# Transposing P through DMA for three of four head groups, and through TensorE into two banks for the last

## The chip, the cores and the metric

The kernel runs on one core of one Trainium2 chip. The metric is the device time of one execution in microseconds (us), as the median of several runs. The kernel before has a median of 2704.88 us in 3 runs (2704.35 to 2705.86).

## The reference

Two layers, and each is an attention block followed by a gated feed-forward block (FFN). The input is x with 2048 tokens of 576 numbers. The attention is recurrent: the tokens come in 64 segments of 32, and each segment sees 8 memory rows ahead of its own 32.

```python
for s in range(64):                                   # layer A, called twice
    h = concatenate([mem, layernorm(x)[32*s:32*s+32]])          # 40 rows
    q, k, v = h @ Wq, h @ Wk, h @ Wv                            # 32 heads of 128
    p = softmax(where(mask, q @ k.T * 128**-0.5, -1e9))         # 40 x 40 for each head
    o = (p @ v) @ Wo
    mem = o[:8]; out[32*s:32*s+32] = o[8:]
x = x + out                                           # then layer B, FFN of width 4608
x = x + (silu(layernorm(x) @ w1) * (layernorm(x) @ w3)) @ w2
```

`mem` of one segment enters the next, so the segments of one layer can't run side by side. Both layers have the same weights.

## The kernel before, in words

**Steps.** Layer 2 runs `LAG = 8` segments behind layer 1, so there are 72 steps, and step `t` works on segment `t` of layer 1 and segment `t - 8` of layer 2. In the 56 steps with both layers (8 to 63) the 40 rows of either layer lie beside each other: 80 columns go through the projections with one load of the weights. In the other 16 steps one layer is there alone. The FFN of four finished segments (128 tokens of one layer, or of both) is cut into 18 pieces that are laid between the attention steps; their weights come by DMA from the queue of SyncE (SP) in two buffers each (`W13`, `W2C`).

**One step.** The 32 heads go in `NG = 4` groups of `GH = 8`. For each group, in the letters of the order (below): `Q` and `q` are the projections to Q and K and their 64-row tails; evictions to `QKT`; `S` the scores, 8 heads by up to two layers, into one bank (layer 1 in partitions 0 to 39, layer 2 in 64 to 103); VectorE (DVE) adds the mask, takes the maximum and subtracts it, ScalarE (ACT) takes the exponential in place (`SME`), DVE sums, inverts, and writes the quotient to `PB` in bf16, each layer's rows at the columns that are the rows of V that they need (`sm_pb`, three or four pieces, as `p_at` says). The other columns of `PB` must be zero.

**The transposition of P** is letter `T` (`ptr`, L1015): eight matmuls of 40 columns with `PB` of one head as the weights and `fold` as the moving operand. `fold` adds the rows of both layers on top of each other, so that one bank holds the sum for all eight heads; two evictions (`pt_ev`, L1022) copy the bank twice to `PTS` and multiply each by a column of `slots`, which is 1 in the partitions of one layer and 0 elsewhere. So the layers are parted again. GpSimd (POOL) then clears that `PB` buffer (`pb_zero`, L1009) once for each group; there are two `PB` buffers and one `PTS`.

**After it**: `P` multiplies V by `PTS` into two banks (`pv`), which are evicted to `OT`; `O` and `o` multiply `OT` by Wo and sum all four groups in one bank (`wo`, `wo_tail`). At the step's end `y_odd`, `y_mem` and `yts` carry the memory rows to the next step's `HT` and the outputs to `YTS`, which letter `p` (`post_tr`) transposes once in four steps. `F`, `f`, `W`, `w` are the FFN, `V`, `v`, `X`, `x`, `G`, `g` the projections to V.

**What sets the order.** `make_nodes` (L232) describes all work as nodes with an engine, a cost, dependencies and buffer slots. The order of TensorE's nodes is written out: `ORDER = FIRST + FOUR * 11 + LAST` (L222), one letter for each node, where `FOUR` holds four steps and repeats eleven times (44 of the 56 steps with both layers). `plan` (L75) takes TensorE's nodes in just that order and lays the nodes of the other engines and the DMAs beside them by its costs; nodes of kind `AD` (evictions) go to ScalarE or VectorE, whichever it finds free first. Each engine then does its own nodes strictly in this order (`ch`, L579): an instruction that waits holds up all that stand behind it on its engine. A matmul node for which the planner chose the mode `col` is issued in two halves of 64 output rows each (`mm`, L586), which changes the number of matmuls and not the work. A change between modes (128 rows, 64 row halves, column halves or quarters) is a change of tile shape on TensorE.

**DMA queues.** Weights and `XN` go out on SP, residuals and results on POOL, and in the kernel before ScalarE issues four DMAs at the very start only.

Of the kernel before, what the change touches and what calls it, by code (L numbers as in the profile page):

```python
# [34 lines left out]
POOLS = {"bank": 8, "qkt": 4, "sme": 2, "pb": 2, "pts": 1, "ot": 4,  # L35
# [158 lines left out]
def ewh(*ns):  # L194
# [5 lines left out]
    "maQQQqqQqqSQqTqSqQQQqSSvVXxPTPTOPOTOoPooOoQqqqqQQSQqqvSVQQTQSqqPQOTSPoXTOPToxPOOooQqqqqQQSQQSvqVQTqqQSQqPSaOTPTO"  # L200
    "PTooPOOooQQqqqqQSQVvSqqQQQqqQTSSPXTOPTOPoToxPOOooQQpQqqVvqqSnQQSfFFqqfQQqSTQqfPFTWPSFTOOooPFTffPOOooWQqqqqQQFSQF"
    "SQffqVvqqQWTQSFxfqfQFSPXTWPFTfOPOTFPOOooooWQqfqQQSFQfqqVvSQqqfFWTQqfQSFPQqfTOSPFOTWPFTOPfoooOoFfqqQQQSWQqqvVSFfq"
    "qQQTWqqSQQPTSOoPbaOTXPxTOPooxOoXqqpQQQSVqqnQvfFSTQqqQQPSFfqqfQTFOPSWTFfPOOTFPWOooooffFQQQqqqWSGFfgqQQqfFSTQPQQqq"
    "qfFSWGTSfgGPFggTGOPOTFPOOooooWVvfqqQQQSFqqffFQQWTSFfqqQPQfqqSFQWTOfPSTaFoOPWOTFPffFOoooWQQqqqqQSbQgqqGSQQTQPQTgq"
    "qSGSOPGggTGPOTOPoooOoQqqppQQQSvqqVnnQQqqSFSffqTFQPQqWTFSPffOwTFPOTFPOWOwooooFffqqQQQSWwQFfgqqGSFqqfQQTWQPQSFffqq"
    "FGTgSwPGfggTGPFTOPOWOOowoooFqqfQQwWQaQfqqSFSvVfqqQFQTFqqfPQTQwSWFSfPOOTFPwTWffFPOOooooWwqqqQQQbSQqqgqGSQTQPQQqgq"
    "TSGSGPggGTOPOTOPoooOo"
)
FOUR = (
    "QqqpQQpQqqVvnSSnQFfqfqFQQQTfqqSFPWTFPSwTfFOOPWTwPOOooooFqqffQQQQfqqSFGSgqfFTQQPwQTQqqqgGSWPFGSfggfFOTGPOwTOPWOoo"  # L210
    "ooFqfqqQQwWQQVqvSaSFFffqqQQwQQqqSTWSFPffTFOPWwTOFPffTOFPwWOooooFfqqqQQWQQSqqqQSQQbQqgqSTGGPSgTGPOTggGPOTwPOOoooo"
)
LAST = (
    "QQpQqqqQSqQpnQqqVvTSSnQFffqqFPQTOwPoSWTffFPFTOPOOoooFqqqfQQwWQQfqfSFSFqGQQqqgTQQPWwFqgfTSSGGPFfggfFTGOPOTWPOOwoF"
    "oooFfqqfQQQwvSqqVQQWQqqSFTSqfqQPQWTOPSwFTFPffOTOwPWOooooFFqqffQQwQQqqvSWVSFqqfQQTWPQTqqSVQvPOSTbOPxwOoTooPOoXqQp"
    "QpqqvVQSQqqnQnSQQqqFTSfqfPQTOPSFTFPOWTOPwOooooFqffqQQQSQQqqqvVSTQQqqFSffqFPQWSwTFPffTOPFOTwPOOoWoooFqfqqQQQFSQfq"
    "xvXVwWSTFPQffqqQWQTSwFFPfqqQOSwWTFOPffTFPOWOwooooFQQvfqqVqqQSQWFSwFffqqQQQSTWQqPqTPSOTOPowOToboPxOoXqqqQQQpSvVqq"
    "qQQSnQTFfqQFSPfqQOSTFfPowTFPfOTOPFOfooowQQqqqfQQSqFSVvqqQwQFTSQffqqQPFTSXPwTOPOTFPOOooooFfxfVvqqQQQSQqqqfQSFQqqq"
    "QSTQwSPFTOffPFTOPwTOPfooOooFQqqqQQSqqqQQSQvVQTSfFQqqPwTFSPfTOFPOTOPoofOoopwFnfffFFwFwfffFFFwffFFwffFFwffFFwfFffF"
    "wFwfffFFFfww"  # L220
# [11 lines left out]
def make_nodes(em, nseg, pools, o=Opt, dma_bw=230e3, load_bw=400e3):  # L232
# [26 lines left out]
    ld_m0 = node("ACT", 0.1, em.load_m0(), prio=-90, name="m0", lat=2.5)  # L259
    ld_t = [load("ldt", kb(3 * R64, 4096), -10.0, em.load_tails(0)), node("ACT", 0.1, em.load_tails(1), prio=-120, name="ldt", lat=6.0)]  # L260
    node("ACT", 0.1, em.load_tails(2), prio=-80, name="ldt", lat=6.0)
# [48 lines left out]
    def v_nodes(name, t, k, prio, tail_at, emit, strips, deps, tail_deps, free):  # L310

        modes = ("col", "quad") if strips[0][3] == R64 else ("c32", "oct")
        b = banks()
        m_ = node("PE", 8 * 0.2158, emit(b, False), deps=deps, prio=prio, mode=modes[0], acq=b, name=name)
        n = node("PE", 0.2158, emit(b, True), deps=deps + tail_deps, prio=prio + tail_at, mode=modes[1], acq=b, name=name + "t")
        reads_ht.setdefault(t, []).extend([m_, n])
        for r in (0, 1):
            outs = em.v_parts(strips, r)
            b[r].users = len(outs)
            for p0, width, row, blk in outs:  # L320
                e = node("AD", (0.49, 0.6), em.v_ev(b[r], p0, width, row, blk), deps=[m_, n] + free.get(blk // 2, []), prio=prio + 0.01 * (blk // 2),
                         rel=[b[r]], name=name + "e")
                vx_ev.setdefault((name, t, blk // 2), []).append(e)
        return [m_, n]
# [16 lines left out]
    def vg_out(t, g, b, deps, row):  # L341

        return [node("AD", (0.49, 0.6), em.v_ev(b[r], row, R64, row, 2 * g + r), deps=deps, prio=t + o.vm + 0.01 * g + (0.05 if row == 0 else 0.0), rel=[b[r]],
                     name="VGe") for r in (0, 1)]

    def vx_pair(t, prio):
# [5 lines left out]
        for k in ((0, 1) if both(t) else (0,)):  # L352
            v_nodes("VX", t, k, prio + 0.01 * k, o.vxt, (lambda k: lambda b, tail: em.vx(t, k, b, tail))(k), em.vx_strips(t, k), deps, [], free)

    def step(t):
# [17 lines left out]
        for g in range(NG):  # L373
# [22 lines left out]
            pb = Slot("pb")  # L396
            d = node("DVE", 0.623 if nl == 2 else 0.606, em.sm_sum(t, g, sme), deps=[c], prio=pf, name="sum")
            w = (1.074 if e else 1.143) if nl == 2 else 0.466
            pbs = node("DVE", w, em.sm_pb(t, g, sme, pb), deps=[d], prio=pf, acq=[pb], rel=[sme], name="pb", lat=0.125 if nl == 2 else 0.225)
            pts = Slot("pts")  # L400
            bt = Slot("bank", users=2)
# [24 lines left out]
            me[f"SC{g}"], me[f"TR{g}"], me[f"PV{g}"], me[f"WO{g}"] = sc, tr, pv, wo  # L426
# [100 lines left out]
    def x_in(g):  # L527
        xn = Slot("xn")
        ld = node("DMA" if g else "ACT", 0.8 if g else 0.1, em.load_xn(g, xn), deps=reads_ht.get(4 * g - 3, [])[:1], prio=4 * g - 3.0 if g else -100, acq=[xn],
                  name="ldxn", lat=2.5)  # L530
# [31 lines left out]
SW = 2 * QW  # L562

# [4 lines left out]
class Emitter:  # L568
# [431 lines left out]
    def sm_pb(self, t, g, sme, pb):  # L1000
        def f(n):
            for kd, key, c0, w in self.p_at(t):
                rs = slice(64 * kd, 64 * kd + QW)
                X, rec = self.T.SME[rs, sme.i], self.T.STAT[rs, sme.i]
                self.v("tensor_tensor", self.T.PB[rs, pb.i, :, c0:c0 + w], X[:, :, key:key + w],
                       rec.unsqueeze(2).to_broadcast([QW, GH, w]), op=ALU.mult)
        return f

    def pb_zero(self, pb):  # L1009
        return lambda n: self.ch("POOL", self.nc.gpsimd.memset(self.T.PB[:, pb.i], 0.0))  # L1010
# [4 lines left out]
    def ptr(self, t, g, pb, b):  # L1015

        def f(n):
            for j in range(GH):
# [3 lines left out]
    def pt_ev(self, t, g, m, b, pts):  # L1022

        def f(n):
            src = self.bk(b)[:, 0:GH * QW]
            if not self.both(t):
                w = 4 * QW
                self.cp(n, self.T.PTS[:, pts.i, 0, m * w:(m + 1) * w], src[:, m * w:(m + 1) * w])
                return
            dst = self.T.PTS[:, pts.i, m, :]  # L1030
            keep = self.T.slots[:, role(t), m ^ role(t):(m ^ role(t)) + 1]
            if n.by == "ACT":
                self.act(dst, src, ACT.Copy, scale=keep)
            else:
                self.v("tensor_scalar", dst, src, keep, None, op0=ALU.mult)
        return f

    def pv(self, t, g, pts, b):
        def f(n):
            nq = self.nq(t)  # L1040
            for j in range(GH):
                self.mm(self.bk(b[j // 4])[:, (j % 4) * nq:(j % 4 + 1) * nq], self.T.V[:, self.head(g, j) // 4, (self.head(g, j) % 4) * E:(self.head(g, j) % 4 + 1) * E],
                        self.T.PTS[:, pts.i, 0:nq // QW, j * QW:(j + 1) * QW], True, True)
        return f

# [66 lines left out]
    def yts(self, t, ls, tail):  # L1112
        def f(n):
            yT, _ = self.yT(t)
            for li in ls:
                j = (t - LAG * li) % 4
                c0 = self.ycol(t, self.kind(t, li), False)
                if not tail:
                    self.cp(n, self.T.YTS[:, li, 0:4, j * SEG:(j + 1) * SEG], yT[:, 0:4, c0:c0 + SEG])
                else:  # L1120
                    self.v("tensor_tensor", self.T.YTS[R64:P, li, 4, j * SEG:(j + 1) * SEG], yT[0:R64, 4, c0:c0 + SEG],
# [3 lines left out]
    def post_tr(self, li, g, b):  # L1125
        def f(n):

            for db in (4, 3, 2, 1, 0):
                d0 = min(db * P, D - P)
                self.mm(self.bk_bf(b, D)[:, d0:d0 + P], self.T.YTS[:, li, db, :], self.T.ident[:, 0:P], True, True, is_transpose=True)  # L1130
# [79 lines left out]
def kernel(  # L1210
# [41 lines left out]
    T.fold = sp.tile([P, QW], BF, name="fold")  # L1252

    T.slots = sp.tile([P, 2, 2], F32, name="slots")

# [13 lines left out]
    T.PB = sp.tile([P, pools["pb"], GH, P], BF, name="PB")  # L1269
# [15 lines left out]
    nc.gpsimd.memset(T.fold[:], 0.0)  # L1285
    for r in (0, R64):
        nc.gpsimd.affine_select(out=T.fold[:], in_=T.fold[:], compare_op=ALU.not_equal, fill=1.0, base=-r,
                                pattern=[[-1, QW]], channel_multiplier=1)

    nc.gpsimd.memset(T.slots[:], 0.0)  # L1290
    for e, kd, lo, hi in ((0, 1, 24, 80), (1, 0, 72, 112)):
        inside, outside = T.slots[:, e, kd:kd + 1], T.slots[:, e, 1 - kd:2 - kd]
        nc.gpsimd.memset(inside, 1.0)
        nc.gpsimd.affine_select(out=inside, in_=inside, compare_op=ALU.is_ge, fill=0.0, base=-lo, pattern=[[0, 1]], channel_multiplier=1)
        nc.gpsimd.affine_select(out=inside, in_=inside, compare_op=ALU.is_ge, fill=0.0, base=hi - 1, pattern=[[0, 1]], channel_multiplier=-1)
        nc.gpsimd.tensor_scalar(outside, inside, -1.0, 1.0, op0=ALU.mult, op1=ALU.add)

# [54 lines left out]
```

## Time and profile before

| | us |
|---|---|
| median of 3 runs (lowest, highest) | 2704.88 (2704.35, 2705.86) |
| the profiled execution | 2708.0 |
| its span, first to last instruction | 2705.0 |
| TensorE (PE) busy in the span | 2618.6 |
| VectorE (DVE) busy | 2097.7 |
| ScalarE (ACT) busy | 1401.6 |
| GpSimd (POOL) busy | 334.1 |

The profiled execution lies 0.1% over the median of the runs. A matmul's busy time in the profile has a modelled end and overlaps that of the next one, so the time that a row of matmuls takes is read as the distance from its start to the start of the next row. All operations are recorded by helpers, so nearly all matmuls have line L591, all ScalarE work L594 and all VectorE work L597; the names of the tiles tell them apart (`bank<-fold,PB` is the transposition of P, `bank<-PTS,V` the product with V, `bank<-QKT` the scores, `bank<-HT,W` Q and K, `bank<-XTB,W` and `bank<-W2C,HTT` the FFN, `bank<-OT,WO` the output projection).

### The profile page before, as it was taken

To read this page: it belongs to the slowest core of one execution; us is meant where nothing else is said; L and a number is where in the kernel's file an instruction comes from. 1 tells how busy PE (TensorE), PEld (TensorE's weight loads), DVE (VectorE), ACT (ScalarE), POOL (GpSimd) and SP (SyncE) were. 2 spreads that over 40 slices of the span, in tenths; PEclk is the share of its full clock that TensorE was granted. 3 is DMA by queue.
4 is the path that set the end of the run, shared out by engine and by line. 5 is a ranking of instruction groups with operands and counts; after the bars stand their busy time and mean duration, and the time that the engine had idled before them with its cause. 6 is when DMAs were issued, how large, how long until landed. Compare 5 with 4: busy or idle time off the path is not lost.

```text
span 2705.0 us, 135792 instructions
## 1 busy us (share of the span) xinstructions
PE 2618.6 (97%) x60482; PEld 2272.3 (84%) x60523; DVE 2097.7 (78%) x5423; ACT 1401.6 (52%) x3978; POOL 334.1 (12%) x411
## 2 busy tenths in 40 slices
PE   5999999999999999999999999999999999999998
PEld 4788888888888888888888888888888888888886
DVE  5777887787788778777877877787777777777876
ACT  2655554554555555554555555455545546554452
POOL 1111110110111011011101101010111101011110
PEclk9999999999999999999999999999999999999999
DMA  9064524244342434434243433423343342334457
GB/s 316 7 182 118 158 82 128 80 119 116 104 124 85 116 90 119 117 108 128 76 119 88 127 108 108 134 80 110 94 124 106 108 139 70 112 93 130 129 166 245
DMA packets 478171, 321.99 MB, mean 119 GB/s; under 512 B 26024, under 2 KB 467760, under 8 KB 476944
## 3 DMA queue, kind: packets, MB, share of 16 engines
q1 hardware_dynamic: 474048, 305.43, 38.5%
q8 instruction: 473, 7.75, 1.2%
q0 software_dynamic: 3024, 6.93, 0.9%
q10 hardware_dynamic: 512, 0.94, 0.2%
q14 instruction: 114, 0.93, 0.1%
HBM read 308.49 MB, written 2.36 MB: 115 GB/s over the span
## 4 chain that ended last, share of the span: by engine, by line
PE 80%; DVE 9%; ACT 6%; issue 2%; DMA 2%; SPq 1%; POOL 0%; ACTq 0%; DVEq 0%; POOLq 0%
PE bank L591 80%; ACT V L594 3%; DVE STAT L597 2%; DVE PTS L597 2%; ACT PTS L594 1%; DVE V L597 1%; DVE SME L597 1%; DVE PB L597 1%; DMA W<-in_A_Wk_dram 1%; DVE HTT L597 1%; SPq L600 1%; DMA W<-in_B_w_dram 1%; ACT HT L594 0%; ACT QKT L594 0%; DMA WV<-in_A_Wv_dram 0%
## 5 line engine op out<-in xcount | busy, mean ns | idle before, releaser
L591 PEld LDWEIGHTS <-W 128*128 128x128 bf16 (+2 forms) x31904 | 1258.2, 100 | 128.8 <-issue 68.7
L591 PE MATMUL bank<-HT,W 128*128 128x80 bf16 (+3 forms) x23040 | 799.9, 196 | 16.8 <-issue 7.3
L591 PE MATMUL bank<-XTB,W 128*64 128x256 bf16 (+5 forms) x8864 | 662.6, 263 | 5.9 <-DMA W<-in_B_w_dram 3.0
L594 ACT ACTIVATE QKT<-bank 128x256 bf16<-128x256 f32 (+2 forms) x1524 | 349.5, 311 | 363.5 <-PE bank L591 320.7
L1010 POOL MEMSET PB<- 128x1024 bf16 x288 | 273.9, 951 | 1944.5 <-PE bank L591 1242.7
L591 PE MATMUL bank<-OT,WO 128*128 128x80 bf16 (+2 forms) x11520 | 401.6, 198 | 2.2 <-issue 1.8
L594 ACT ACTIVATE V<-bank 32x512 bf16<-32x512 f32 (+1 forms) x609 | 347.8, 586 | 90.4 <-PE bank L591 81.6
L591 PEld LDWEIGHTS <-WO 128*128 128x128 bf16 (+1 forms) x11520 | 376.8, 102 | 13.7 <-issue 4.4
L591 PE MATMUL bank<-WV,HT 128*32 128x512 bf16 (+5 forms) x3728 | 362.3, 381 | 3.8 <-issue 2.2
L591 PE MATMUL bank<-W2C,HTT 128*128 128x288 bf16 (+1 forms) x2776 | 318.4, 286 | 2.9 <-issue 1.8
L597 DVE TENSOR_REDUCE STAT<-SME 104x8 f32<-104x320 f32 (+1 forms) x576 | 274.0, 476 | 25.2 <-ACT SME L594 18.9
L597 DVE TENSOR_TENSOR PB<-SME,STAT 40x128 bf16<-40x128 f32 (+4 forms) x912 | 275.5, 336 | 9.7
L594 ACT ACTIVATE HTT<-bank 128x512 bf16<-128x512 f32 (+1 forms) x324 | 175.3, 550 | 185.9 <-PE bank L591 183.9
L591 PEld LDWEIGHTS <-HT 128*32 128x32 bf16 (+4 forms) x3768 | 164.1, 99 | 119.5 <-issue 20.3
L597 DVE SCALAR_TENSOR_TENSOR XR<-bank,XR 128x288 f32<-128x288 f32 x576 | 243.7, 448 | 23.3 <-PE bank L591 17.4
L591 PEld LDWEIGHTS <-HTT 128*128 128x128 bf16 (+1 forms) x2840 | 222.4, 103 | 42.2 <-issue 4.5
L597 DVE SCALAR_TENSOR_TENSOR HTT<-HTT,bank 128x512 bf16<-128x512 bf16 (+1 forms) x324 | 201.0, 620 | 59.0 <-ACT HTT L594 56.2
L594 ACT ACTIVATE OT<-bank 128x320 bf16<-128x320 f32 (+1 forms) x392 | 147.0, 403 | 173.0 <-PE bank L591 146.3
L597 DVE CAST QKT<-bank 128x192 bf16<-128x192 f32 (+4 forms) x524 | 140.5, 315 | 117.7 <-PE bank L591 117.3
L597 DVE TENSOR_TENSOR HTT<-HTT,bank 128x512 bf16<-128x512 bf16 (+1 forms) x324 | 203.6, 628 | 28.5 <-PE bank L591 0.9
L594 ACT ACTIVATE PTS<-bank,slots 128x320 bf16<-128x320 f32 x315 | 157.0, 531 | 128.8 <-PE bank L591 95.0
L594 ACT ACTIVATE SME<-SME 104x320 f32<-104x320 f32 (+1 forms) x288 | 135.5, 470 | 100.2 <-DVE SME L597 95.5
(69 smaller groups left out, 1856.8 us busy)
## 6 DMA issues: line engine op xcount, KB each, us to landing
W<-in_B_w_dram SPq DMA_DIRECT2D x612, 256.0 KB, 3.6
W2C<-in_B_w_dram SPq DMA_DIRECT2D x306, 288.0 KB, 3.3
W<-in_B_w_dram SPq DMA_DIRECT2D x612, 32.0 KB, 3.5
W<-in_B_w_dram SPq DMA_DIRECT2D x8, 1024.0 KB, 12.2
W<-in_A_Wq_dram SPq DMA_DIRECT2D x9, 512.0 KB, 9.5
WO<-in_A_Wo_dram SPq DMA_DIRECT2D x4, 1152.0 KB, 16.7
XR<-in_A_x_dram POOLq DMA_DIRECT2D x16, 288.0 KB, 2.8
WV<-in_B_w_dram SPq DMA_DIRECT2D x4, 1152.0 KB, 10.9
```

The lines of the kernel that those rows point to most:

```text
L591: self.ch("PE", self.nc.tensor.matmul(out, lhsT=lhsT, rhs=rhs, start=start, stop=stop, skip_group_check=True, **k))
L594: self.ch("ACT", self.nc.scalar.activation(*a, **k))
L597: self.ch("DVE", getattr(self.nc.vector, fn_)(*a, **k))
L600: self.ch("SP", self.nc.sync.dma_start(out=out, in_=in_))
L1010: return lambda n: self.ch("POOL", self.nc.gpsimd.memset(self.T.PB[:, pb.i], 0.0))
```

## The change

In the 56 steps with both layers, the groups 0, 1 and 2 lose their `T`. In its place ScalarE's queue issues one DMA (`ptd`) that reads 112 partitions of `PB` (224 KB for the eight heads) and writes them transposed to `PTS`, and `P` takes the columns of the two layers out of `PTS` by a stepped access pattern (`pcols`). Group 3, and all groups of the 16 steps with one layer, keep the matmuls, now with the identity and without the folding: 80 columns for each head in place of 40, four heads to a bank, and so two banks, each evicted by a plain copy. `fold` and `slots` are gone. There is now one `PB` buffer and two of `PTS`. As the layers' rows stand at the same columns in all groups of a step, `PB` is cleared once in a step (71 times) and no longer 288 times; the clearing waits for the last transposition of the step before, and the first write of `PB` waits for the clearing. `YO` now lies in unused rows of `YTS`. Some costs of the planner are changed (evictions of V, the first loads), and the three strings of the order are new throughout.

```diff
-POOLS = {"bank": 8, "qkt": 4, "sme": 2, "pb": 2, "pts": 1, "ot": 4,
+DMA_GROUPS = 3
+TRD, TRL = 1.41, 2.6
+POOLS = {"bank": 8, "qkt": 4, "sme": 2, "pb": 1, "pts": 2, "ot": 4,
...
 FOUR = (
...
+    "QQppQqqqVQqvSnSnQFffqqFQQQqqfSFPWFPSwffOOFPwTOPWOooooFqffqQQFQQqqSWwFSGqfqgQQwPQQqqgSGWPGFSffggFGOPOTOPwOooooFqq"
+    "fqQQvVSQQQqfqWSFFfqqqQQQWSwSFPffPFOwOWPFffTOPFOowoWooFqqqfQQWSQQQqqqQbaSwGSQQqqggGPGSPgOOGPgTOPoooOo"
...
+            if g == 0 and t:
+                zero = [node("POOL", 0.95, em.pb_zero(pb), deps=last_pt, prio=pf, acq=[pb], name="pbz")]
...
-            tr = node("PE", 8 * 0.0258, em.ptr(t, g, pb, bt), deps=[pbs], prio=pf + o.tr, mode="full/col", acq=[pts, bt], name="TR")
-            node("POOL", 0.95, em.pb_zero(pb), deps=[tr], prio=pf, rel=[pb], name="pbz")
-            pe_ = [node("AD", (0.425, 0.46) if nl == 2 else ew(160), em.pt_ev(t, g, m, bt, pts), deps=[tr], prio=pf, rel=[bt], name="PTe") for m in (0, 1)]
+            if nl == 2 and g < DMA_GROUPS:
+                pe_ = [node("ACT", TRD, em.ptd(t, g, pb, pts), deps=[pbs], prio=pf, acq=[pts], rel=[pb], name="TRD", lat=TRL)]
+                last_pt[:] = pe_
+            else:
+                bt = banks(nl)
+                tr = node("PE", 8 * (0.0258 if nl == 1 else 0.0358), em.ptr(t, g, pb, bt), deps=[pbs], prio=pf + o.tr, mode="full/col", acq=[pts] + bt, rel=[pb], name="TR")
+                pe_ = [node("AD", ew(320), em.pt_ev(t, g, i, b, pts), deps=[tr], prio=pf, rel=[b], name="PTe") for i, b in enumerate(bt)]
+                last_pt[:] = [tr]
...
+    def ptd(self, t, g, pb, pts):
+        return lambda n: self.ch("ACT", self.nc.scalar.dma_start(out=self.T.PTS[:, pts.i], in_=self.pbt(pb)[0:PQ].rearrange("p h k -> p (h k)"),
+                                                                 transpose=True))
...
-                self.mm(self.bk(b)[:, j * QW:(j + 1) * QW], self.T.PB[0:104, pb.i, j, :], self.T.fold[0:104, :], True, True)
+                k = j * nq % (4 * SW)
+                self.mm(self.bk(b[j * nq // (4 * SW)])[:, k:k + nq], self.pbt(pb)[0:104, j, :], I, True, True)
...
-            if n.by == "ACT":
-                self.act(dst, src, ACT.Copy, scale=keep)
-            else:
-                self.v("tensor_scalar", dst, src, keep, None, op0=ALU.mult)
+            nq = self.nq(t)
+            h = GH * QW // nq
+            self.cp(n, self.T.PTS[:, pts.i, h * i:h * (i + 1), 0:nq], self.bk(b)[:, 0:4 * SW].rearrange("p (h q) -> p h q", h=h))
...
-    T.PTS = sp.tile([P, pools["pts"], 2, GH * QW], BF, name="PTS")
+    T.PTS = sp.tile([P, pools["pts"], GH, PQ], BF, name="PTS")
-    T.YO = sp.tile([R64, 2 * QW], F32, name="YO")
-    T.YTS = sp.tile([P, 2, 5, P], BF, name="YTS")
+    T.YTS = sp.tile([P, 10, P], BF, name="YTS")
+    T.YO = T.YTS[0:R64, 8:10, :].rearrange("p a b -> p (a b)").bitcast(F32)[:, 0:2 * QW]
```

More of the change, by code (lines that the diff above doesn't have):

```diff
@@ L1042, in f, with pcols @@
                 self.mm(self.bk(b[j // 4])[:, (j % 4) * nq:(j % 4 + 1) * nq], self.T.V[:, self.head(g, j) // 4, (self.head(g, j) % 4) * E:(self.head(g, j) % 4 + 1) * E],
-                        self.T.PTS[:, pts.i, 0:nq // QW, j * QW:(j + 1) * QW], True, True)
+                        self.pcols(t, g, pts, j), True, True)
         return f
+    def pcols(self, t, g, pts, j):
+        P_ = self.T.PTS[:, pts.i, j, :]
+        if not self.both(t) or g >= DMA_GROUPS:
+            return P_[:, 0:self.nq(t)]
+        v, e = P_[:, 0:1], role(t)
+        return bass.AP(v.tensor, v.offset + R64 * e, [list(x) for x in v.ap][:-1] + [[R64 - P * e, 2], [1, QW]])
     def ot_ev(self, t, g, ab, b, ot):
@@ L1284 @@
                             pattern=[[-1, P]], channel_multiplier=1)
[L1285 to L1296, printed above, removed]
     nc.gpsimd.memset(T.maskb[:], 0.0)
```

82 lines of the change are left out of this document (39 added, 43 removed).

## The prediction, made before the changed kernel ran

> **What bounds the kernel now.** I read the page first, then busy time by stretches, the chain that ended last, TensorE's waits, and the timeline of one step for prices.
>
> ```profile
> span 2705.0 us, 135792 instructions
> PE 2618.6 (97%) x60482; PEld 2272.3 (84%) x60523; DVE 2097.7 (78%) x5423; ACT 1401.6 (52%) x3978; POOL 334.1 (12%) x411
> ```
> ```profile
> 640.00:2200.00 1560.00, 1541.25 (x34144) 1351.25 (x34172) 1230.90 (x3154) 829.11 (x2313) 184.44 (x219) 1.00 0.38 108
> ```
> ```profile
> PE 80%; DVE 9%; ACT 6%; issue 2%; DMA 2%; SPq 1%; POOL 0%; ACTq 0%; DVEq 0%; POOLq 0%
> ```
>
> The second line gives length, then busy time of PE, PEld, DVE, ACT and POOL, granted clock, DMA share and GB/s. In the long middle TensorE is busy 1541 of 1560 us (99%) at full clock (1.00): a matmul that goes saves its time, as long as nothing makes TensorE wait instead. The chain says that this isn't free: 15% of it runs through VectorE and ScalarE, so the softmax chain often ends only just in time.
>
> ```profile
> PE bank L591 <- ACT PTS L594: 12.3, 20, 1.9
> PE bank L591 <- DMA XTB<-in_A_mem_dram: 10.5, 1, 10.5
> PE bank L591 <- DMA W<-in_A_Wk_dram: 7.6, 3, 4.6
> PE bank L591 <- DVE PTS L597: 5.4, 20, 1.0
> ```
>
> These are TensorE's waits (us in total, times, longest). For the transposed P it waits 17.7 us in 40 of 288 groups; two start-up loads cost 18.1.
>
> **The change part by part.** First the matmuls. The time of a row is the distance to the start of the next kind.
>
> ```profile
> L591 PE MATMUL bank<-fold,PB 104*128 104x40 bf16 (+1 forms) x2792 | 109.9, 182 | 2.9 <-DVE PB L597 2.3 <-POOL PB L1010 0.2
> ```
> ```profile
> 1307.34 1.31 PE L591 MATMUL bank<-OT,WO 128*128 128x80 bf16 x32
> 1308.48 0.36 PE L591 MATMUL bank<-fold,PB 104*128 104x40 bf16 x8
> ...
> 1312.48 0.36 PE L591 MATMUL bank<-fold,PB 104*128 104x40 bf16 x8
> 1312.69 1.14 PE L591 MATMUL bank<-W2C,HTT 128*128 128x288 bf16 x8
> 1314.45 0.45 PE L591 MATMUL bank<-PTS,V 128*128 128x80 bf16 x8 [0.63 <-ACT PTS L594]
> 1314.74 3.15 PE L591 MATMUL bank<-OT,WO 128*128 128x80 bf16 x96
> ...
> 1331.55 1.92 PE L591 MATMUL bank<-XTB,W 128*128 128x256 bf16 x16
> 1333.31 3.60 PE L591 MATMUL bank<-HT,W 128*128 128x80 bf16 x96
> 1336.75 0.36 PE L591 MATMUL bank<-fold,PB 104*128 104x40 bf16 x8
> 1337.04 0.39 PE L591 MATMUL bank<-XTB,W 64*128 64x256 bf16 x4
> 1337.27 0.45 PE L591 MATMUL bank<-HT,W 64*128 64x80 bf16 x16
> 1337.65 0.40 PE L591 MATMUL bank<-QKT 128*64 128x40 bf16 x15
> ```
> ```profile
> 1337.89 0.19 PE L591 MATMUL bank<-QKT 128*64 128x40 bf16 x1
> 1337.92 1.91 PE L591 MATMUL bank<-XTB,W 128*64 128x256 bf16 x31
> ...
> 1340.89 0.43 PE L591 MATMUL bank<-fold,PB 104*64 104x40 bf16 x15
> 1341.14 0.28 PE L591 MATMUL bank<-XTB,W 128*64 128x256 bf16 x1
> ...
> 1343.24 1.12 DVE L597 TENSOR_TENSOR PB<-SME,STAT 40x128 bf16<-40x128 f32 x4
> ...
> 1343.40 0.30 PE L591 MATMUL bank<-W2C,HTT 128*64 128x288 bf16 x1
> ...
> 1344.42 0.45 PE L591 MATMUL bank<-fold,PB 104*64 104x40 bf16 x16
> ```
>
> A group of eight transposing matmuls takes 0.21 us (1312.48 to 1312.69), in column halves 0.25 (1340.89 to 1341.14). The 2792 matmuls are 227 groups of 8 and 61 of 16: 227 x 0.21 + 61 x 0.25 = 62.9 us. The changed kernel's order has 1024: 58 whole and 6 halved groups of 40 columns, 54 whole and 2 halved of 80. Eight matmuls of 80 columns take 0.29 (1314.45 to 1314.74), halved 0.33 by the same surcharge: 58 x 0.21 + 6 x 0.25 + 54 x 0.29 + 2 x 0.33 = 30.0. **Saved: 32.9 us.** By the 109.9 us of the group's own busy time, where ends overlap the next work, it would be half as much again; that is an upper end and I don't use it.
>
> Against it stands the new order: tile shapes change 1128 times in it, 1081 before (counted in both). A group ahead of another shape takes 0.29 (1336.75 to 1337.04) where one ahead of the same takes 0.21, so a change costs 0.08, and 47 of them **3.8 us**. That other kinds are more often issued in halves costs nothing: 16 half FFN matmuls `W` take 1.02 us (1343.40 to 1344.42), eight whole ones at most 1.14. Net -29.1 us on TensorE.
>
> Now the new wait. From the end of the scores (1337.89 + 0.19) to P written (1343.24 + 1.12) pass 6.3 us, sums on VectorE and the exponential with all that stands between them. Then before: `T`, one eviction, `P`. After: one DMA of T us, from the start of its issue to its landing. How much matmul work lies between `S` and `P` of the same group follows from the letters. In the first step of the new `FOUR`, behind the third `S`, stands `FPWFPSwffOOF` and then its `P`: three `F` at 1.76 (1331.55 to 1333.31), two `P` at 0.29, two `W` at 1.02, one `S` at 0.27 (1337.65 to 1337.92), two `f` at 0.23 (1337.04 to 1337.27), two `O` at 1.14 (1307.34 to 1308.48), together 10.9 us. Worked out so, the twelve DMA groups of the four repeated steps have room for 17.6, 14.8, 10.2; 14.2, 10.3, 12.0; 12.6, 15.1, 10.9; 9.9, 12.2, 12.4 us. TensorE waits where 6.3 + T is over the room. Over all 14 x 4 steps with both layers this sums to 0 us for T = 3.6, 11 for 4.1, 32 for 4.6, 55 for 5, 116 for 6. (A wait also gives later groups room, so these are rather too high; 6.3 is one group, and a longer chain would be as bad as a longer T.)
>
> ```profile
> W<-in_B_w_dram SPq DMA_DIRECT2D x612, 256.0 KB, 3.6
> W<-in_B_w_dram SPq DMA_DIRECT2D x612, 32.0 KB, 3.5
> W<-in_B_w_dram SPq DMA_DIRECT2D x8, 1024.0 KB, 12.2
> ```
> ```profile
> 0.81 0.60 ACTq L603 DMA_DIRECT2D W<-in_A_Wk_dram  x1
> 1.45 0.83 ACTq L603 DMA_DIRECT2D XN<-in_A_x_dram  x1
> ```
>
> No transposing DMA is in the trace. It can't land sooner than the small load (3.5 us); the far end is the 12.2 us of the 1,024 KB load. The nearest row is the load of 256 KB with 3.6, against 224 KB here. I take **T = 4.1**: that row and half a microsecond for loads already under way (0.38 of the DMA time is taken in the middle) and for the eviction that may stand ahead on ScalarE. So **11.2 us of new waits**, and the sum is -32.9 + 3.8 + 11.2 = **-17.9 us**. The planner's own 1.41 and 2.6 in the diff aren't used for this.
>
> [...]
>
> **What is moved or queued.** On ScalarE the 168 issues cost 0.6 to 0.83 us each by the rows, 100 to 140 us; were the engine held until landing, 690. It is idle 48% of the span, and sheds evictions:
>
> ```profile
> L594 ACT ACTIVATE PTS<-bank,slots 128x320 bf16<-128x320 f32 x315 | 157.0, 531 | 128.8 <-PE bank L591 95.0 <-DVE PTS L597 23.7 <-ACT V L594 7.1
> ```
>
> In the new order 81 of these 315 evictions are left to it. But order matters more than load: behind the DMA, which waits for P, stand the FFN's tanh, the next group's exponential and evictions of Q and K; if VectorE is late with P, they are late too, and TensorE waits for a bank. On VectorE the write of P waits for the landing of the group before, since there is one `PB`; behind it stand the next mask addition and the FFN's products. POOL's memset goes from 288 to 71 times, at the turn of a step, where 19 us of matmuls lie between the scores of group 3 and those of the next step: nothing. SP: its DMAs and ScalarE's take eight semaphores in turn, so 157 of the 168 wait first for a weight load eight DMAs earlier, and 157 load pieces wait for a DMA of P. By the order two of the twelve repeated groups depend on a load that starts 1.8 and 3.6 us after the scores; it lands 3.6 later, at 5.4 and 7.2, against P at 6.3, where the room is 14.8 and 15.1. Cost nothing, and up to the 0.9 us if that room shrinks. Added traffic is 168 x 224 KB = 38.5 MB, or 14 GB/s on the 108 of the middle; hidden, unless a load that has 1.2 us of slack meets it (11 such). `YO` inside `YTS`: one more dependency of `post_tr`, once in four steps, hidden by the step between; bound 5 us. The start: 24 dummy matmuls become 12 inside the wait for `W`; I cost it at nothing, between the 7.6 us of that wait and as much loss.
>
> **How the sum stands to the median.** The profiled execution took 2708.0 us, its span 2705.0; -17.9 gives 2687.1 and 2690.1. The median of the runs is 2704.9, 0.1% under the profiled one; by the same difference it becomes **2687**.
>
> **Rivals.**
> 1. *The DMA takes the place of the eviction as the last to end (slower).* One mechanism: `P` stands in TensorE's fixed order behind a landing that comes later than the work laid in between covers. The point is T = 4.5, where the waits reach 29.1 us. At T = 6 they are 116: 2704.9 - 29.1 + 116 = 2792. For it: the room is under 11 us in four of twelve groups, and the chain grows by more than 3 us (4.1 in place of 0.21 and an eviction of 0.53). Against it: the new order has given the shortest room 9.9 us.
> 2. *Gain given back (no change).* With one `PB` the second group's P is written only after T and 1.1 us (its own writing) from the first. The scores follow at 5.2 us, so from T = 4.1 VectorE stands still once a step; at T = 4.6 that is 0.5 x 56 = 28 us on an engine 78% busy, and the waits above are 32: 2704.9 - 29.1 + 32 = 2708.
> 3. *The DMA doesn't transpose at the pace of a load.* If its blocks go one after another, T is nearer the 12.2 us row; room is short in all groups, by 70 us in four steps: 14 x 70 = 977, 3650 us. [...]
>
> **How the numbers follow.** Forecast 0.56, rival 1 0.27, rival 2 0.10, rival 3 0.07. A measurement of this kernel tells about 0.2% (5.4 us) from no change. Faster is the forecast, 0.56; same rival 2, 0.10; slower 0.34. The forecast's own range runs from 2660 (T = 3.6, the start-up wait and half of the 17.7 us for P gone too: 2704.9 - 29.1 - 7.6 - 8.8) to 2699. The whole range goes up to T = 5.5 (83 us of waits): 2758. Beyond it are rival 3, the worse part of rival 1 (0.10) and 0.03 below.
>
> **What would show it.** Right: `ident,PB` x1024 with about half the busy time of 109.9; TensorE's waits for a DMA into `PTS` under 15 us; landing under 4.4 us; the middle stretch again 99% busy. Wrong: landing of 5 us or more, and `DMA PTS` at the top of TensorE's waits; or waits for `QKT`, `V`, `OT` by ScalarE grown, since its queue stood at a DMA; or the DMA's issue holding ScalarE for microseconds.

## The result, and the profile after

The changed kernel takes 2737.8 us (median; 2728.66 to 2739.38 in 4 runs), against 2705.37 us for the kernel before on the same chip: ratio 1.0113, 95% interval 1.0100 to 1.0126. It is slower by 1.1%, where 0.7% faster was forecast. The profiled execution took 2739.38 us, its span 2737.5.

The page of the changed kernel, the same rows as were shown of before: engines, and shares of the chain that ended last.

```profile
span 2737.5 us, 133454 instructions
...
PE 2604.8 (95%) x59438; PEld 2252.7 (82%) x59468; DVE 2115.2 (77%) x5471; ACT 1216.6 (44%) x3530; POOL 129.3 (5%) x182
...
PE 67%; DMA 14%; DVE 11%; ACT 3%; issue 3%; SPq 1%; ACTq 0%; POOL 0%; DVEq 0%; POOLq 0%
PE bank L603 67%; DMA PTS<-PB 11%; DVE PB L609 3%; DVE SME L609 2%; DVE STAT L609 2%; ACT V L606 1%; DMA W<-in_B_w_dram 1%; SPq L612 1%; DVE V L609 1%; DVE XR L609 1%; DVE HTT L609 1%; DMA W<-in_A_Wk_dram 1%; DVE QKT L609 1%; DMA WO<-in_A_Wo_dram 0%; ACT QKT L606 0%
```

TensorE is busy 14 us less and the span is 32 us longer, so about 46 us more of it are idle. TensorE's share of the chain falls from 80% to 67%, and a new link, the DMA from `PB` to `PTS`, has 11%. The middle stretch (length, busy time of PE, PEld, DVE, ACT and POOL, clock, DMA share, GB/s), in the changed kernel:

```profile
640.00:2200.00 1560.00, 1503.38 (x32862) 1313.17 (x32878) 1232.21 (x3178) 675.28 (x1968) 72.35 (x99) 0.99 0.50 124
```

TensorE is busy 96% of it, not 99%. Here are the stretches in which both layers run, from the first mask addition of step 8 to that of step 64, first before, then after:

```profile
244.00:2427.00 2183.00, 2153.14 (x48163) 1883.26 (x48196) 1724.65 (x4426) 1159.13 (x3263) 259.13 (x306) 1.00 0.38 109
```
```profile
239.00:2465.00 2226.00, 2141.63 (x47083) 1863.35 (x47108) 1743.61 (x4496) 974.04 (x2850) 101.68 (x138) 0.99 0.50 124
```

This **stretch** is 43 us longer: idle time grows from 29.9 to 84.4 us, and busy time falls by 11.5. All of the loss lies here. The changed kernel reaches step 8 five us sooner (239 against 244) and takes six less after step 64 (272.3 us to the end, against 278.4). These two differences aren't put down to the change: the kernels of the experiments with the changed order and full loads reach step 8 at 236.0 to 244.2 and take 273.1 to 278.1 us after step 64. Now who waits in the changed kernel, TensorE first, then VectorE (us in total, times, longest):

```profile
PE bank L603 <- DMA PTS<-PB: 50.1, 32, 3.5
...
PE bank L603 <- DVE PB L609: 10.0, 14, 3.1
```
```profile
DVE HTT L609 <- ACT HTT L606: 99.3, 97, 3.1
...
DVE PB L609 <- DMA PTS<-PB: 76.6, 56, 3.2
```

Two engines wait for the same landing: TensorE, because `P` needs `PTS`, and VectorE, because it may not write the one `PB` again before the DMA has read it. The DMA itself, by its landing time, counted from the start of its issue (median us), ScalarE's queue (packets, MB, share of the DMA engines' time), and its issue there (ns, least, median, most):

```profile
PTS<-PB ACTq DMA_TRANSPOSE x168, 4.4
...
q10 hardware_dynamic: 156416, 39.50, 9.9%
```
```profile
L1028 ACTq DMA_TRANSPOSE PTS<-PB x168: 1237/1242/2468, 243.4 to 2448.5; - x168
...
DMA to landing us min/median/max: 2.6/4.4/7.4
```

The median landing, 4.4 us, is near the predicted 4.1. But the prediction took one value for all 168, and they spread from 2.6 to 7.4. One place shows what a late one does, in the step that begins a repeated four (start, us, engine, the instruction, and in brackets the idle time before it and what ended it):

```profile
1183.26 0.22 PE L603 MATMUL bank<-QKT 128*64 128x40 bf16 x2
...
1187.94 9.76 SPq L612 DMA_DIRECT2D W<-in_B_w_dram  x9
...
1189.36 1.24 ACTq L1028 DMA_TRANSPOSE PTS<-PB  x1
...
1191.22 0.20 DVE L609 RECIPROCAL STAT<-STAT 104x8 f32<-104x8 f32 x1
...
1192.48 0.69 DVE L609 TENSOR_TENSOR HTT<-HTT,bank 128x512 bf16<-128x512 bf16 x1
...
1194.84 1.12 DVE L609 TENSOR_TENSOR PB<-SME,STAT 40x128 bf16<-40x128 f32 x4 [1.68 <-DMA PTS<-PB]
...
1196.00 1.24 ACTq L1028 DMA_TRANSPOSE PTS<-PB  x1
...
1201.83 0.48 PE L603 MATMUL bank<-PTS,V 128*64 128x80 bf16 x16 [2.77 <-DMA PTS<-PB]
1201.88 1.13 DVE L609 TENSOR_TENSOR PB<-SME,STAT 40x128 bf16<-40x128 f32 x4 [1.33 <-DMA PTS<-PB]
```

Group 0's DMA starts at 1189.36 beside nine pieces of weight loads. Group 1's divisor is ready at 1191.42 and VectorE is through with its FFN product at 1193.17, but stands 1.68 us until group 0 has landed, at 1194.84. Only then is group 1 written; its scores had ended at 1183.48 (the first line), so P stands 12.5 us behind them, where the prediction has 6.3. Its DMA starts at 1196.00 and lands 5.8 us later, and TensorE, out of work, waits 2.77 us for it. Group 2 is held up in its turn. So one late landing delays the next group's DMA, which the prediction had priced as two separate matters.

### The profile page after: what moved, and what is told of

Read it like the earlier page. It is cut to its first block, busy times and chain, and to the rows that moved or that the text cites. A ratio compares the mean times of both kernels' runs of the same rounds, so it can differ in the third digit from the quotient of the medians.

```text
span 2737.5 us, 133454 instructions
## 1 busy us (share of the span) xinstructions
PE 2604.8 (95%) x59438; PEld 2252.7 (82%) x59468; DVE 2115.2 (77%) x5471; ACT 1216.6 (44%) x3530; POOL 129.3 (5%) x182
## 2 busy tenths in 40 slices
DMA packets 634065, 360.40 MB, mean 132 GB/s; under 512 B 181928, under 2 KB 623664, under 8 KB 632848
## 3 DMA queue, kind: packets, MB, share of 16 engines
q10 hardware_dynamic: 156416, 39.50, 9.9%
## 4 chain that ended last, share of the span: by engine, by line
PE 67%; DMA 14%; DVE 11%; ACT 3%; issue 3%; SPq 1%; ACTq 0%; POOL 0%; DVEq 0%; POOLq 0%
PE bank L603 67%; DMA PTS<-PB 11%; DVE PB L609 3%; DVE SME L609 2%; DVE STAT L609 2%; ACT V L606 1%; DMA W<-in_B_w_dram 1%; SPq L612 1%; DVE V L609 1%; DVE XR L609 1%; DVE HTT L609 1%; DMA W<-in_A_Wk_dram 1%; DVE QKT L609 1%; DMA WO<-in_A_Wo_dram 0%; ACT QKT L606 0%
## 5 line engine op out<-in xcount | busy, mean ns | idle before, releaser
L603 PE MATMUL bank<-HT,W 128*128 128x80 bf16 (+3 forms) x23040 | 794.8, 197 | 17.9 <-ACT HT L606 6.4
L606 ACT ACTIVATE QKT<-bank 128x256 bf16<-128x256 f32 (+2 forms) x1488 | 338.5, 317 | 337.1 <-PE bank L603 324.6
L603 PE MATMUL bank<-OT,WO 128*128 128x80 bf16 (+3 forms) x11520 | 411.6, 199 | 2.7 <-DMA WO<-in_A_Wo_dram 1.1
L603 PE MATMUL bank<-WV,HT 128*32 128x512 bf16 (+4 forms) x3827 | 369.7, 384 | 4.4 <-issue 1.4
L606 ACT ACTIVATE V<-bank 64x512 bf16<-64x512 f32 (+1 forms) x545 | 309.6, 585 | 107.4 <-PE bank L603 73.4
L609 DVE TENSOR_TENSOR PB<-SME,STAT 40x128 bf16<-40x128 f32 (+4 forms) x912 | 275.7, 336 | 85.3 <-DMA PTS<-PB 76.6
L603 PE MATMUL bank<-W2C,HTT 128*64 128x288 bf16 (+1 forms) x3264 | 328.5, 290 | 1.2 <-DMA W2C<-in_B_w_dram 0.7
L603 PEld LDWEIGHTS <-HTT 128*64 128x64 bf16 (+1 forms) x3328 | 237.0, 107 | 34.2 <-issue 2.7
L609 DVE SCALAR_TENSOR_TENSOR XR<-bank,XR 128x288 f32<-128x288 f32 x576 | 243.9, 448 | 17.9 <-PE bank L603 13.3
L606 ACT ACTIVATE OT<-bank 128x320 bf16<-128x320 f32 (+1 forms) x370 | 138.3, 401 | 250.4 <-PE bank L603 231.8
L609 DVE CAST V<-bank 64x512 bf16<-64x512 f32 (+1 forms) x319 | 216.9, 686 | 34.4 <-PE bank L603 28.0
L609 DVE CAST QKT<-bank 128x256 bf16<-128x256 f32 (+2 forms) x560 | 152.8, 316 | 52.6 <-PE bank L603 49.9
L603 PE MATMUL bank<-PTS,V 128*64 128x80 bf16 (+3 forms) x2976 | 130.3, 200 | 61.3 <-DMA PTS<-PB 50.1
## 6 DMA issues: line engine op xcount, KB each, us to landing
W<-in_B_w_dram SPq DMA_DIRECT2D x8, 1024.0 KB, 12.2
WV<-in_B_w_dram SPq DMA_DIRECT2D x4, 1152.0 KB, 10.7
```

What stands on the lines that cost most here:

```text
L603: self.ch("PE", self.nc.tensor.matmul(out, lhsT=lhsT, rhs=rhs, start=start, stop=stop, skip_group_check=True, **k))
L606: self.ch("ACT", self.nc.scalar.activation(*a, **k))
L609: self.ch("DVE", getattr(self.nc.vector, fn_)(*a, **k))
```

## Experiments

The letters are those of the recorded expectations. Theory A: the weight loads share the DMA engines with the transposing DMAs and stretch their landing. Theory B: the single `PB` couples VectorE to the landing, and its standing still in its fixed order delays the next group. Theory C: the transposition itself is what takes long. Theory D: the new order is the worse one by itself. Without a letter, the plain reading: `P` is late for the landing, and TensorE's waits there are the loss. A, B and C can hold together. The stretch is the time from step 8 to step 64 as above; 2182.3 us before, 2225.9 after.

**1. Weight loads cut.** `e1_quiet_after` is the changed kernel, `e2_quiet_before` the kernel before, both with FFN weight loads that bring 16 of 128 partitions (the rest of the weights is left out).

```diff
-self.dma(W[:, 4 * kind:4 * kind + 4], wd[0:4 * P, ...].rearrange("(c p) f -> p c f", p=P))
+self.dma(W[0:16, 4 * kind:4 * kind + 4], wd[0:4 * P, ...].rearrange("(c p) f -> p c f", p=P)[0:16])
```

> The changed kernel, but every FFN weight load before the last four brings 16 of 128 partitions (the rest of the weights is zero; the number of DMAs, their semaphores and all waits stay). Theory A, the weight loads share the DMA engines with the transposing DMAs and stretch their landing: median landing under 3.2 us (4.4 now), TensorE's waits for it under 5 us (50.1 now), the half-speed clock records in the stretch with both layers mostly gone, time 2670 to 2690. Theory B, the single buffer PB chains two landings: shorter landings help it too, so it can't be told from A by this run alone. Theory C, the transposition itself is what takes long: landing stays at 4 us and more, time over 2725.

> The kernel before with the same cut of the FFN weight loads (16 of 128 partitions, the rest zero). All theories: TensorE waited 3 us for these loads, so 2695 to 2706; if it is faster than that, part of what the run of the changed kernel with the same cut gains is not the transposition's.

Measured: 2646.48 us (2645.64 to 2647.86), ratio to before 0.9777 (0.9762 to 0.9791); the control 2691.24, ratio 0.9943 (0.9925 to 0.9960). Both are faster than was expected (2670 to 2690, and 2695 to 2706). The control gained 14 us where at most 10 was expected, all of it outside the stretch (2182.9 us). Against that control the change is worth -44.8 us. TensorE's middle, the landing, and VectorE's wait in `e1_quiet_after`:

```profile
640.00:2200.00 1560.00, 1544.14 (x34049) 1354.72 (x34047) 1271.32 (x3281) 701.43 (x2046) 73.98 (x101) 1.00 0.19 39
```
```profile
PTS<-PB ACTq DMA_TRANSPOSE x168, 3.2
```
```profile
DVE PB L609 <- DMA PTS<-PB: 8.9, 13, 1.5
```

So with the DMA engines 19% busy in the middle in place of 50% the same DMA lands in 3.2 us (2.6 to 5.6), VectorE's wait falls from 76.6 to 8.9 and TensorE's from 50.1 to 2.8, and TensorE is busy 99% of the middle. Theory A holds: 1.2 us of the median landing come with the weight loads. Theory C as the only cause falls by its line (4 us and more). Theory D falls: with early landings the new order is the better one. The stretch of the control, then of `e1_quiet_after`, each from its own step 8 to its own step 64:

```profile
238.88:2421.79 2182.91, 2157.02 (x48183) 1883.72 (x48177) 1724.07 (x4423) 1159.54 (x3262) 259.13 (x306) 1.00 0.08 21
```
```profile
233.53:2375.11 2141.58, 2119.54 (x47105) 1853.32 (x47097) 1739.90 (x4495) 974.94 (x2848) 101.86 (x138) 1.00 0.19 39
```

It is 41.3 us shorter. TensorE's busy time falls by 37.5, which is 8 more than the prediction's net 29.1 (one 3.41 us record at half clock in the control can be 1.7 of it). Idle time falls by 3.9 only: the 14.3 us for which TensorE waits for the evictions to `PTS` in the control's stretch go, and other short waits take most of their place.

**2. Two `PB` in turn.** The plan and the order stay; to make room, the last two heads use the output weights of the thirtieth, so that two heads of `WO` are left out.

```diff
-    T.PB = sp.tile([P, GH, P], BF, name="PB")
+    T.PB = sp.tile([P, 2, GH, P], BF, name="PB")
...
             pb = Slot("pb")
+            pb.turn = g % 2
...
-        return self.T.PB[:]
+        return self.T.PB[:, pb.turn]
```

> The changed kernel with two PB buffers in turn, its order of instructions unchanged; the clearing covers both; to make room, the last two heads use the output weights of the thirtieth. Theory B: VectorE's wait for landings (76.6 us in 56 times) goes, TensorE's wait in group 1 of every fourth step goes (26.9 of 50.1 us), with some of the half-speed clock records: 2695 to 2715. Theory A without B: landings stay at 4.4 us and TensorE's waits over 40 us, time 2728 to 2740.

Measured: 2690.39 us (2688.38 to 2700.41), ratio 0.9949 (0.9934 to 0.9965), stretch 2173.7. The landing is unchanged. TensorE's waits in `e3_two_pb`:

```profile
PE bank L604 <- DMA PTS<-PB: 23.6, 21, 2.4
...
PE bank L604 <- DMA W<-in_B_w_dram: 7.0, 13, 0.9
```
```profile
PTS<-PB ACTq DMA_TRANSPOSE x168, 4.4
```

VectorE's wait for the landing is gone, TensorE's is halved, its wait in group 1 of every fourth step falls from 26.9 to 0.3 us, and 47 us of the time go, more than was expected (2695 to 2715): theory B. What is left, 23.6 us at a median landing of 4.4, is as much as the prediction's own list of rooms gives between 11 us at T = 4.1 and 32 at 4.6; how far this is luck is said below.

**3. TensorE doesn't wait for the landing.** `P` reads a piece of `W` in place of `PTS` where the DMA transposes, so the product is not that of P; the DMA and VectorE's wait for it stay.

```diff
-        v, e = P_[:, 0:1], role(t)
+        v, e = self.T.W[:, 0, j * PQ:j * PQ + 1], role(t)
```

> The changed kernel, but in the 168 DMA groups the product with V takes a piece of W in place of PTS (P is left out there), so TensorE never waits for a landing; the DMAs run, and VectorE still waits for them before it writes the one PB again. If the loss is TensorE's wait for the landing: 50 us of waits and 10 us or more of half-speed clock go, 2665 to 2690. If VectorE's standstill costs by itself, through the mask additions and FFN products behind it: over 2700.

Measured: 2731.33 us (2724.71 to 2746.52), ratio 1.0103 (1.0070 to 1.0135). Of the two expectations the second came (over 2700): 50 us of TensorE's waits were taken away, and the time is 6 us lower, which the two intervals don't tell from nothing. The waits in `e5_no_landing_wait`, TensorE's and VectorE's:

```profile
PE bank L603 <- DVE PB L609: 17.7, 24, 3.1
...
PE bank L603 <- DVE SME L609: 11.2, 14, 1.5
PE bank L603 <- DMA W<-in_B_w_dram: 10.4, 13, 2.0
```
```profile
DVE PB L609 <- DMA PTS<-PB: 87.5, 63, 3.8
```

TensorE now waits for VectorE's other work, which stands behind the write of `PB`. This refutes the plain reading as a cause by itself: the wait at `P` is where the delay shows, not where it comes from.

**4. A plain copy in place of the transposing DMA**, between the same tiles (112 by 896 elements, 196 KB; P isn't transposed).

```diff
-dma_start(out=self.T.PTS[:, pts.i], in_=self.pbt(pb)[0:PQ].rearrange("p h k -> p (h k)"), transpose=True)
+dma_start(out=self.T.PTS[0:PQ, pts.i].rearrange("p h k -> p (h k)"), in_=self.pbt(pb)[0:PQ].rearrange("p h k -> p (h k)")[:, 0:GH * PQ])
```

> The changed kernel with a plain copy of the first 112 partitions by 896 columns in place of the transposing DMA (196 KB in place of 224; P is not transposed). Theory C: landing falls by 1 us or more, the issue from 1.24 to 0.6 us, time under 2715. Theories A and B: landing 3.5 to 4.5 us and the waits with it nearly as now, time 2720 to 2740.

Measured: 2660.40 us (2657.88 to 2667.66), ratio 0.9825 (0.9807 to 0.9842), stretch 2150.9. The DMA in `e4_plain_dma`:

```profile
q10 hardware_dynamic: 22016, 34.67, 4.1%
...
PTS<-PB ACTq DMA_DIRECT2D x168, 196.0 KB, 3.1
```
```profile
L1028 ACTq DMA_DIRECT2D PTS<-PB x168: 517/518/614, 241.0 to 2371.3; - x168
```

The plain copy moves an eighth less (196 KB for 224) in a seventh of the packets, and lands 1.3 us sooner. Landing is counted from the start of the issue, and the issue takes 0.52 us in place of 1.24, so 0.72 of the 1.3 us are in the issue. The time falls by 77 us, all of the loss and more: theory C holds beside A, as to where the lateness is from, and B says how it becomes a loss; A and B without C fall by the recorded line (2720 to 2740). The run changes three things at once (the transposing, the issue that goes with it, and an eighth of the bytes), and what each is worth isn't shown.

**5. Matmuls in place of some DMAs.** `T` in its two-bank form goes back into the changed kernel's order, some 2 us ahead of `P`, in all 168 groups (`e6_all_matmul`) or only at chosen places (t % 4, g) of the repeated four steps.

```diff
+def by_dma(t, g):
+    return g < 3 and (t % 4, g) not in ((0, 1), (2, 2))
...
-            if nl == 2 and g < DMA_GROUPS:
+            if nl == 2 and by_dma(t, g):
...
-    "QQppQqqqVQqvSnSnQFffqqFQQQqqfSFPWFPSwffOOFPwTOP
+    "QQppQqqqVQqvSnSnQFffqqFQQQqqfSFTPWFPSwffOOFPwTOP
```

> The changed kernel with no DMA group: a T is put into its order some 2 us ahead of each of the 168 P, in the two-bank form of the last group. Theory D, the new order is the worse one by itself: 2740 and more. If the DMA is the loss: no wait for landings, but 168 groups at 0.29 us and a change of shape for many, 50 to 65 us more of work: 2715 to 2745, with TensorE's idle time back near 90 us (132.7 now).

> The changed kernel, but in the two places of the four-step pattern that hold 40.8 of the 50.1 us of waits (group 1 of steps 0, 4, 8 ..., group 2 of steps 2, 6, ...; 28 of 168 groups) the DMA is replaced by T in two banks, put into the order 2.8 us ahead of P. If single DMAs in a tight place, with the one PB ahead of them, are the loss: waits for landings under 15 us, 10 us of work more, 2690 to 2708. If the landings are too late everywhere: the waits move to other groups, 2725 and more.

> The same with group 2 of steps 0, 4, 8 ... as a third place (42 of 168 groups). It takes away 5.6 us more of waits and adds 5 us of work: within 8 us of the run with two places.

| places by matmul | groups | us (lowest, highest) | ratio to before (95%) | TensorE / VectorE wait for landing, us |
|---|---|---|---|---|
| none (the changed kernel) | 0 | 2737.8 (2728.66, 2739.38) | 1.0113 (1.0100, 1.0126) | 50.1 / 76.6 |
| (0,1), (2,2) | 28 | 2716.13 (2710.90, 2719.69) | 1.0033 (1.0020, 1.0046) | 24.9 / 58.7 |
| (0,1), (0,2), (2,2) | 42 | 2704.49 (2699.21, 2707.55) | 0.9993 (0.9984, 1.0003) | 6.8 / 37.8 |
| (0,0), (2,2) | 28 | 2706.54 (2702.32, 2711.57) | 1.0001 (0.9990, 1.0012) | 27.3 / 44.0 |
| (0,0), (0,1), (2,2) | 42 | 2711.80 (2705.82, 2720.88) | 1.0027 (1.0013, 1.0042) | 23.9 / 37.3 |
| (0,0), (0,1), (0,2), (2,2) | 56 | 2690.47 (2690.03, 2691.78) | 0.9943 (0.9927, 0.9959) | 7.5 / 14.0 |
| all | 168 | 2777.18 (2774.40, 2778.05) | 1.0262 (1.0247, 1.0278) | none |

With no DMA at all this order is the slowest of all, and by the recorded line its time is that of theory D (2740 and more). TensorE's busy time grows by 53.6 us, as expected (50 to 65), but its idle time falls to 117.9 us only, where near 90 was expected: it waits for VectorE now (24.0 us for `HTT`, 11.2 for `SME`). The order was laid out for groups that need neither a place for `T` nor a bank; that this is the reason wasn't tried. So the run says that this order needs its DMAs, and by experiment 1 it isn't worse with them. Two places miss what was expected (2690 to 2708, and under 15 us of waits for landings): 17.4 us of waits have moved on to (0,2). Three places gain 11.6 us on two, where at most 8 was expected. In the two kernels of the fourth and fifth row the place was chosen by theory B: the 26.9 us for which TensorE waits at (0,1) should come from the landing of group 0, ahead of it.

> Like the run with the matmuls at two places, but at group 0 of every fourth step (t % 4 = 0) in place of group 1, and again at group 2 of t % 4 = 2: 28 of 168 groups by TensorE. Theory that VectorE stands before the one PB: the 26.9 us for which TensorE waited at (0, 1) came from the landing of group 0, which holds up the write of group 1; without a DMA at (0, 0) they fall under 8 us and VectorE's 20.9 us behind the landing of (0, 0) go; with 13.9 us at (2, 2) gone too and 28 x 0.3 = 8 us of matmuls more, 2685 to 2715 us, below the 2716 of the other two places. Rival that only the landing at (0, 1) itself is too late for P: the waits there stay over 20 us and the time is 2720 to 2735.

> Matmuls at groups 0 and 1 of t % 4 = 0 and at group 2 of t % 4 = 2 (42 of 168). Theory of the one PB: VectorE's waits for a landing fall under 25 us, TensorE's under 10 us; 2680 to 2710 us. Rival, that matmuls put into this order cost as much as the waits that they spare (0.3 us each, a change of tile shape and two evictions more): not under the 2704 of the three places tried first.

> Matmuls at all three groups of t % 4 = 0 and at group 2 of t % 4 = 2 (56 of 168). If waits still count, 2675 to 2705 us; if the added matmuls now cost more than the few waits that are left, slower than the kernel with 42 of them by 3 to 10 us.

With a matmul at (0,0) the DMA at (0,1) isn't waited for by TensorE at all, as theory B has it, and its mean landing falls from 5.3 to 3.4 us; the time is in the expected range, and the kernel is 10 us faster than with as many matmuls at (0,1) and (2,2). But 22.8 us of waits stand at (0,2) in place of some 5.5: there the landing takes 6.1 us now, and the delay has moved on by one group. Taking out (0,1) too leaves 18.4 us there and adds 14 groups of matmuls; that kernel isn't under the 2704 us of the third row, as the rival had it, and misses what theory B expected: 2680 to 2710 us, and TensorE's waits under 10 us (23.9) and VectorE's under 25 (37.3). Only with the whole step by matmul does the wait go. The last of them, `e8_matmul_at_four`, is in its expected range and faster than the changed kernel and the one before, by 0.6% against before. Its largest waits of TensorE:

```profile
PE bank L623 <- DVE XN L629: 13.6, 1, 13.6
PE bank L623 <- issue: 10.4, 15, 2.0
PE bank L623 <- DVE PB L629: 8.5, 13, 3.1
PE bank L623 <- DMA PTS<-PB: 7.5, 6, 3.0
```

## Why the prediction was wrong

**The matmuls: right, and 8 us too small.** `T` with the identity is 1024 matmuls, as counted. Their own busy time, in the changed kernel:

```profile
L603 PE MATMUL bank<-ident,PB 104*128 104x40 bf16 (+3 forms) x1024 | 50.1, 193 | 12.1 <-DVE PB L609 10.0 <-ACT OT L606 1.1 <-ACT V L606 1.0
```

That is about half of 109.9, and where the waits are gone (`e1_quiet_after` against its control) TensorE's busy time falls by 37.5 us, not 29.1. A part that the sum left out, the 17.7 us that TensorE had waited for the old evictions, belongs on the same side; the prediction used half of it only for the low end, and in the quiet pair other waits take most of its place.

**The new waits: the step that failed.** The sum put 11.2 us there, and nothing for VectorE's waits; measured are 50.1 us of TensorE's and 76.6 of VectorE's. It had T = 4.1 everywhere and a fixed 6.3 us from the scores to the written P. Its rule, that TensorE waits where this chain and T together are over the room, fits the place with most of the waits, as shown below; its two constants don't. T is 2.6 to 7.4 us, and its mean by place (t % 4, g) 3.1 to 6.0. The 6.3 us was one group: measured in the same way, the median by place is 4.6 to 10.7 us in `e3_two_pb`, where VectorE never waits for a landing, and 10.7 at (0,1), where the scores of two groups stand close behind each other. The trace of the kernel before has 10.7 there too, so this could have been read from it. In the changed kernel it is 12.3, since VectorE's wait for the landing of group 0 comes on top, and T is 5.3: together 17.6 us where the list of rooms has 15.1 (the list begins with the third of the four steps). That is 2.5 us too many, and TensorE waits there 11 times for 2.4 us on average. So 26.9 of TensorE's 50.1 us stand at a place to which the sum gave none. With two `PB` the DMA there starts sooner and its mean landing is 3.3 us: 10.7 and 3.3 are under 15.1, and 0.3 us of waits are left.

The list of rooms, with the measured median of 4.4 in it, gives some 24 us, nearly the 23.6 of the kernel with two `PB`. That is in part luck: it puts 11 us at (1,0), 7 at (2,2) and 6 at (3,1), where that kernel has 3.5, 12.0 and none.

What makes the rest is rival 2's mechanism. The prediction named it, said that from T = 4.1 "VectorE stands still once a step", and priced it, at T = 4.6, at 28 us on an engine 78% busy, of which nothing entered the time. The profile has 56 such waits and 76.6 us of them, though not one in each step: 24 stand behind DMAs of each fourth step (t % 4 = 0) and 19 behind those of t % 4 = 2. Taking them away is worth 47 us of the time: 2737.8 with one `PB`, 2690.4 with two, against a forecast of 2687. That the last two lie so near is luck as well: of the 18.4 us between the spans of the kernel before and that with two `PB` (2705.0 and 2686.6), 8.6 lie in the stretch, where the forecast has all of its 17.9.

**Rival 1**, slower by the landing at `P`, gave the sign, and its point of T = 4.5 lies beside the 4.4 measured. But its price there is no change, 33 us short of what was measured, and as one mechanism alone it falls by experiment 3. **Rival 3** falls: the longest landing is 7.4 us, and the median far from the 12.2 us row. The smallest is 2.6, below the 3.5 that the prediction held for the least.

**The 256 KB row was the wrong neighbour.** That weight load lands in 3.6 us; the plain copy of experiment 4 lands in 3.1 and the transposing one in 4.4. So the two copies differ by 1.3 us of landing, 0.72 of it in the issue, with an eighth fewer bytes in the plain one. That a transposing DMA lands like a load was the prediction's estimate, and no run shows it.

**What was costed at nothing.** ScalarE's queue: an issue took 1.24 us in the median, more than the 0.6 to 0.83 of the estimate, and all of them 231; 138 of the evictions to `PTS` are left on ScalarE, where the prediction had 81. ScalarE is idle 56% of the span and its queue has 0% of the chain. Each of the 168 DMAs starts at most 0.37 us after its P is written, so neither the queue nor the shared semaphores held them up; what the longer issue costs ScalarE's other work, no run here tries alone. The weight loads aren't late for the added traffic (the load of 256 KB lands in 3.7 us, 3.6 before). The start, the memset and `YO` were not tried by themselves.

**What stays open.** Of the 29.1 us that TensorE's busy time should have lost in the stretch, 11.5 are seen, where the quiet pair shows 37.5. Stretches at half clock (below) explain up to 15.4 of the missing 17.6; the rest is not settled. How theories A, B and C share the loss is open too: each of the three runs takes away more than the 32 us of the loss, and none joins two of them. Nor is it tried whether a kernel with two `PB` and all heads' weights can be made: the second `PB` takes 2,048 bytes of each partition, for which that run left out two heads of `WO` (2,304 bytes).

## What to carry to other kernels

The same DMA landed in 3.2 us in the median when little else moved and in 4.4 beside the weight loads: price a landing as a spread, quiet to crowded, and sum the waits over that spread. Read the chain ahead of it at each place of the order, not at one. A buffer that a DMA reads must be free before the next writer, so count the waits of the engine that writes it in order as well as of the one that reads the result: with a single buffer a late landing starts the next transfer late (VectorE waited 76.6 us for landings with one `PB` here, and not at all with two). And take away a wait in an experiment before believing its number: the 50 us at `P` gave back about 6.

## What the runs showed of the hardware

**TensorE's clock falls to half behind some of its waits.** Three stretches of 3 us of the changed kernel around the wait of 3.41 us that ended at 726.21, and two at one of 2.40 us that ended at 2171.65 (the granted clock is the third number from the right):

```profile
722.00:725.00 3.00, 0.80 (x15) 0.53 (x10) 2.04 (x5) 0.13 (x1) 0.00 (x0) 1.00 0.82 176
725.00:728.00 3.00, 1.79 (x41) 1.80 (x43) 1.70 (x6) 0.77 (x2) 0.00 (x0) 0.59 0.02 4
728.00:731.00 3.00, 3.00 (x57) 2.44 (x54) 2.62 (x7) 0.95 (x2) 0.00 (x0) 0.85 0.66 148
2171.00:2174.00 3.00, 2.35 (x30) 2.02 (x31) 2.23 (x6) 0.86 (x3) 0.08 (x1) 0.79 0.93 276
2174.00:2177.00 3.00, 3.00 (x45) 2.85 (x43) 1.98 (x6) 0.78 (x3) 0.87 (x1) 0.64 0.08 22
```

The trace records the granted clock in pieces that begin and end on a grid of 3.41 us (to 0.005 us in the traces of the kernel before and the changed one, but for the last piece). The stretch with both layers has 8 records at half clock in the changed kernel, seven of 3.41 us and one of 6.83, and none in the kernel before; `e3_two_pb` has one, `e1_quiet_after` and `e4_plain_dma` have none. Together they are 30.7 us, so 15.4 us of lost time at most: a price of waiting on top of the wait that no sum of waits holds. Six of them stand behind waits for a landing (1.99 to 3.51 us long), one behind a wait of 2.57 for VectorE, one behind two waits of 0.57 and 0.96 for a weight load. The length of a wait doesn't decide: those of 2.77 us at 1201.83 and 3.10 us at 1843.43 have none behind them. Cut into the windows of the grid, they leave TensorE idle for no more than 1.86 us of one window, and the wait of 1.99 us at 564.85 lies whole in one. In the stretches of all 13 traces, each of the 21 windows with TensorE idle for 1.99 us or more is followed by half clock; of those below, 11 in more than 8,000 are. Seven of the 21 are in the changed kernel, idle for 1.99 to 2.87 us, where 2 of its other 645 windows are followed by half clock; in the kernel before no window is idle for more than 0.89 us. So in these stretches a window idle for 1.99 us was enough, and the one of 1.86 was not.

**The transposing form moves its data in small packets.** ScalarE's queue, with its few loads at the start, has 156,416 packets and 9.9% of the DMA engines' time, where the plain copy has 22,016 and 4.1%. The changed kernel has 155,904 more packets under 512 bytes than the kernel before (181,928 and 26,024 by the pages), 928 for each of the 168 DMAs of 224 KB, or 247 bytes each on average.
